# First pair's q and k in three parts, a new order of the attention steps, and the last block copied whole

## The chip, the cores and the metric

One core of one Trainium2 chip runs the whole program. The metric is the time of one execution in device microseconds (us). The engines are named as in the profile: PE (TensorE; PEld its weight loads), DVE (VectorE), ACT (ScalarE), POOL (GpSimd) and SP (SyncE, which issues most DMAs).

## The reference

```python
# q, k, v: (2, 12, 448, 64) f32; tokens 2*448 = 896, d_model 12*64 = 768
scores = q @ k.T / 8;  causal mask;  attn = softmax(scores);  a = attn @ v
x = a.transpose(0, 2, 1, 3).reshape(896, 768)
h = x @ w_in            # 768 x 2048, float64 in memory
x = max(0.01 * h, h) @ w_out          # 2048 x 768
xn = x / sqrt(mean(x*x) + 1e-6) * rms_g
y = (silu(xn @ w_gate) * (xn @ w_val)) @ w_out2    # 768 x 1536, twice, and 1536 x 768
```

## The kernel before, in words

Every product that needs more than fp32r is made of three products of a high and a low part (`prod`, L150). After the attention the program is a long chain of such matmuls on PE: x·w_in, g·w_out, the gated pair, and the last product (L626 to L656), which leaves the output in 14 blocks of 128 rows x 384 columns. Weights come as float64 and are decoded by ACT, DVE and POOL (L96 to L145).

The attention works on 12 pairs of heads (p = 0 to 11). Its steps are small functions, one entry each in a dictionary; the string `ORDER` (L40) lists them, and the program is emitted in that order, engine by engine in first-in-first-out queues. A name is a letter for the step, the pair, and a part; what follows an @ is the engine (A for ACT, D for DVE, P for POOL). The steps that matter here:

- `q`, `k`: load of a pair's q or k into a tile `n` (four buffers). For pair 0 (`PLAIN`, L32) the load, the turn and the copy go by parts: `load_part` (L255), `turn_part` (L265), `copy_part` (L271), with `PARTS` (L34) naming the chunks of 128 rows in each part; q comes through ACT's queue, k through SP's (L263).
- `tq`, `tk`: PE transposes into PSUM (L269 for pair 0, L306 and L309 otherwise; the tile is `qk`, three buffers). `hq`, `hk`: the copy to SBUF (`F`; L275 for pair 0, L315 otherwise). `lq`, `lk`: the low part, on DVE (L319).
- `s`: scores on PE (L331 for pair 0, L345 otherwise; four PSUM buffers). `m`: mask and row maximum on DVE (L353). `e`: exponential on ACT (L362). `g`, `i`, `n`: guard (L367), inverse (L371), normalisation (L375).
- `t`, `c`: PE transposes of the probabilities (`pt`, L382) and their copies (`pT`, L395). `x`: times v on PE (L404). `f`: copy (L412) and low part (L414) of the result; x has one PSUM buffer, so x of pair p waits for f of pair p-1.
- `b`, `d`, `v`: loads of tails of q (tile `qe`, L287), tails of v (`ve`, L291) and of v (`vn`, L282). `w`, `y`, `z`: decode and first matmuls (L421 to L423) of the w_in product, placed among the attention steps. `w0.0` is the DMA of the first 768 KB of w_in (tile `raw`, L104).
- `~n`: n matmuls on a constant tile that only keep PE at work (`keep_busy`, L510); the order of before has none, but 13 stand ahead of the first step (L514). The constant tile `pace` is set by a DVE memset (L86).

Of the kernel before, what the change touches and what calls it, by code (L numbers as in the profile page):

```python
# [37 lines left out]
ORDER = """  # L40
q0a k0a tk0a q0b tq0a hk0a@A tq0b hq0a@A k0b tk0b k1 s0.0 hk0b@A hq0b@A q1 b0 m0.0 s0.2 q2 s0.6 tk1 m0.1 e0.1
k2 m0.3 e0.0 m0.2 g0.0@P m0.6 tq1 e0.3 hk1@A hq1@A i0.0 s0.4 tq2 e0.6 lk1 g0.6@P lq1 m0.4 m0.5 e0.2 hq2@A s1.0
i0.6 lq2 m1.4 m1.0 e0.4 e0.5 m1.1 s1.2 n0.6@P g0.2@P tk2 q3 i0.2 m1.2 hk2@A t0.3 e1.0 c0.3@A k3 tq3 s1.6 lk2
n0.1@P g0.4@P n0.0@P tk3 n0.2@P m1.5 i0.4 q4 tq4 n0.3@P n0.4@P hq3@A e1.4 m1.6 s2.2 d0 m1.3 hk3@A k4 lq3 lk3
hq4@A q5 m2.2 v0 s2.0 e1.3 lq4 b1 e1.6 n0.5@P e1.5 t0.1 c0.1@A k5 t0.2 s2.6 c0.2@A t0.0 e1.1 e1.2 tk4 tq5 m2.4
m2.0 m2.5 m2.1 m2.3 m2.6 s3.2 g1.0@D i1.0 n1.4@D n1.5@D s3.0 hk4@A c0.0@A e2.3 e2.2 m3.2 q6 hq5@A x0 n1.3 n1.2
n1.6@P n1.0 m3.3 lk4 m3.0 t1.3 n1.1 t1.1 e2.0 e2.1 e2.4 m3.5 lq5 m3.1 t1.0 e2.5 e2.6 c1.0@A f0.0@A s3.6 c1.3@D
c1.1@D g2.0@D m3.4 t1.2 tk5 e3.3 tq6 i2.0 s4.0 c1.2@A e3.5 m3.6 n2.5@D hq6@A f0.1 hk5@D n2.4@P n2.3 s4.2 n2.1
x1 e3.1 n2.6@P n2.0 e3.4 q7 m4.0 lk5 n2.2 m4.3 e3.2 e3.6 e4.3 t2.3 m4.5 v1 k6 lq6 m4.1 k9 t2.1 t2.2 e3.0 c2.3@A
m4.4 c2.2@A s4.6 t2.0 w0.0 c2.1@D e4.0 g3.0@P e4.5 c2.0@A d1 q8 f1.0@D m4.2 tk6 i3.0 tq7 hk6@A s5.0 n3.4@P m4.6  # L50
f1.1 e4.4 hq7@D s5.2 n3.6@P m5.1 e4.2 x2 n3.2 lk6 n3.3 e4.1 e4.6 lq7 m5.4 m5.2 n3.5@P n3.1 g4.0@D m5.0 k7 t3.2
n3.0 i4.0 f2.0@A w0.1@P e5.1 e5.4 n4.2 t3.3 n4.0 t3.1 s5.6 c3.2@D c3.3@A n4.6@P c3.1@A f2.1 m5.5 e5.2 tk7 t3.0
hk7@A c3.0@A w0.2 m5.3 m5.6 t4.3 s6.0 m6.0 k8 c4.3@A s6.2 e5.0 n4.4@P e5.6 e5.3 w1.0 n4.3 n4.5@P w0.3 n4.1 lk7
e5.5 x3 t4.1 f3.0@A v2 m6.4 m6.2 w0.4 g5.0@P m6.5 m6.1 i5.0 f3.1 m6.3 n5.1 n5.0 e6.4 c4.1@A s6.6 t4.2 t4.0 tk9
c4.2@A s7.6 c4.0@A hk9@A tk8 tq8 q9 e6.5 m7.6 m6.6 lk9 s7.0 hk8@A e6.0 e6.3 k10 s7.2 hq8@A m7.0 m7.2 n5.3
n5.6@P n5.4@P n5.2 n5.5@P e6.6 e6.2 e6.1 e7.0 x4 lk8 lq8 f4.0@A t5.0 m7.1 m7.4 e7.6 m7.5 w0.5@P t5.3 c5.3@A
t5.1 c5.0@D c5.1@A s8.6 g6.0@D m7.3 f4.1 e7.3 e7.5 t5.2 tq9 i6.0 m8.6 c5.2@D e8.6 e7.4 n6.4@P s8.0 n6.5@P s8.2
n6.1 m8.2 n6.3 n6.0 e7.2 m8.4 m8.3 n6.2 m8.0 hq9@A e7.1 k11 x5 q11 q10 t6.0 n6.6@P lq9 m8.5 m8.1 c6.0@A t6.1
t6.3 t6.2 c6.3@A g7.0@P f5.0@D c6.2@A e8.1 c6.1@D i7.0 f5.1 s9.0 n7.4@D m9.5 m9.4 w0.6 m9.0 s9.2 n7.5@P e8.5
e8.0 e8.2 x6 tq10 tk10 e8.4 v3 m9.1 m9.3 e9.5 e8.3 n7.3 g8.0@P s9.6 hq10@A y0.0 tq11 n7.1 n7.0 m9.2 i8.0 lq10  # L60
f6.0@A hk10@A e9.3 y0.1 n7.2 lk10 n8.0 e9.2 n7.6@D e9.0 hq11@D t7.1 n8.2 n8.5@P lq11 n8.1 n8.3 n8.4@P w1.1@P
t7.3 m9.6 s10.6 c7.1@A y0.2 c7.3@A t7.0 f6.1 t7.2 tk11 y0.3 c7.0@D t8.2 y0.4 e9.6 c7.2@A e9.4 m10.6 w1.2 w1.3
e9.1 t8.1 g9.0@P y0.5 s10.0 z0.0 c8.1@A c8.2@A i9.0 s10.2 hk11@D w1.4 lk11 m10.0 n9.4@P n8.6@P z0.1 w1.5@P x7
m10.1 m10.2 n9.1 t8.0 t8.3 e10.6 m10.4 e10.0 e10.4 n9.2 n9.6@P e10.2 c8.3@A m10.5 s11.6 f7.0@D n9.3 f7.1 s11.0
m10.3 c8.0@A m11.6 s11.2 w1.6 x8 e10.3 m11.5 e10.1 m11.4 e10.5 g10.0@D n9.5@P e11.5 e11.6 i10.0 m11.0 m11.1
t9.3 n10.6@D n9.0 e11.0 c9.3@D n10.4@P e11.4 w2.0 t10.3 y1.0 n10.1 n10.0 t9.2 g11.4@D e11.1 c10.3@A c9.2@A
n10.5@P n10.2 n10.3 y1.1 t9.0 m11.3 f8.0@D i11.4 g11.0@D t9.1 g11.6@D f8.1 i11.6 t10.0 c9.1@A y1.2 w2.1@P
c9.0@D x9 m11.2 t10.2 e11.3 z0.2 w2.2 e11.2 n11.6@P g11.2@P c10.0@D i11.2 f9.0@D f9.1 t10.1 c10.2@A i11.0
n11.4@P t11.3 y1.3 c10.1@A n11.3@P c11.3@D x10 f10.0@A n11.2@P n11.5@P n11.0@D n11.1@P t11.2 t11.1 c11.2@A
t11.0 c11.1@A c11.0@A y1.4 y1.5 z1.0 f10.1 x11 f11.0@A z1.1 w2.3 f11.1 w2.4 z1.2  # L70
"""
# [615 lines left out]
```

## Time and profile before

| | |
|---|---|
| median of 3 runs | 589.68 us (589.66 to 590.01) |
| the profiled execution, its own time | 591.03 us |
| its span, first to last instruction | 589.1 us |
| PE busy | 583.2 us (99%) |
| DVE, ACT, POOL busy | 389.6, 265.1, 49.9 us |
| attention, on PE | from the start to about 96 us |

In the rows, a time is the start in us from the span's start, the next number how long it lasted; in brackets stands how long the engine had been idle and who ended it. `x8` is a count. SPq and ACTq are DMA issues of those engines. Rows of the chain of waits have start, length, and what was waited for.

### The profile page before, as it was taken

To read this page: it belongs to the slowest core of one execution; us is meant where nothing else is said; L and a number is where in the kernel's file an instruction comes from. 1 tells how busy PE (TensorE), PEld (TensorE's weight loads), DVE (VectorE), ACT (ScalarE), POOL (GpSimd) and SP (SyncE) were. 2 spreads that over 40 slices of the span, in tenths; PEclk is the share of its full clock that TensorE was granted. 3 is DMA by queue.
4 is the path that set the end of the run, shared out by engine and by line. 5 is a ranking of instruction groups with operands and counts; after the bars stand their busy time and mean duration, and the time that the engine had idled before them with its cause. 6 is when DMAs were issued, how large, how long until landed. Compare 5 with 4: busy or idle time off the path is not lost.

```text
span 589.1 us, 8454 instructions
## 1 busy us (share of the span) xinstructions
PE 583.2 (99%) x3265; PEld 532.7 (90%) x3265; DVE 389.6 (66%) x703; ACT 265.1 (45%) x521; POOL 49.9 (8%) x105
## 2 busy tenths in 40 slices
PE   8999999999999999999999999999999999999997
PEld 6778878999999999999999999999999999999997
DVE  6989996766666556555655998788787796840000
ACT  6989884444444433332333743434434444420000
POOL 4455570000000000000000000000000000000000
PEclk9999999999999999999999999999999999999999
DMA  7893313433333322333234254344343351721001
GB/s 160 188 219 73 92 55 105 118 110 110 112 121 108 111 92 90 107 106 128 90 107 112 104 160 151 114 132 139 108 145 124 108 160 55 193 75 41 28 27 41
DMA packets 83688, 65.07 MB, mean 110 GB/s; under 512 B 35648, under 2 KB 80576, under 8 KB 83648
## 3 DMA queue, kind: packets, MB, share of 16 engines
q1 hardware_dynamic: 82544, 64.21, 37.7%
q8 instruction: 26, 0.43, 0.3%
q10 hardware_dynamic: 1104, 0.33, 0.2%
q14 instruction: 14, 0.11, 0.1%
HBM read 61.77 MB, written 2.75 MB: 110 GB/s over the span
## 4 chain that ended last, share of the span: by engine, by line
PE 96%; DMA 2%; DVE 1%; SPq 0%; issue 0%; ACTq 0%; ACT 0%
PE mm L541 17%; PE mm L153 10%; PE mm L155 10%; PE mm L154 10%; PE mm L559 7%; PE mm L560 7%; PE mm L558 7%; PE mm L639 5%; PE mm L641 5%; PE mm L640 5%; PE x L404 4%; PE pt L382 3%; PE s L345 3%; DMA n<-in_q_dram 1%; PE qk L306 1%; DMA qe<-in_q_dram 0%
## 5 line engine op out<-in xcount | busy, mean ns | idle before, releaser
L153 PE MATMUL mm<-a,hi 128*128 128x448 f32 x300 | 109.7, 366 | 0.0
L154 PE MATMUL mm<-a,lo 128*128 128x448 f32 x300 | 109.6, 365 | 0.0
L155 PE MATMUL mm<-a,hi 128*128 128x448 f32 x300 | 109.6, 365 | 0.0
L134 ACT CAST hi<-we 128x768 fp32r<-128x768 f32 (+1 forms) x58 | 47.2, 815 | 131.9 <-PE mm L541 53.9
L140 DVE TENSOR_TENSOR lo<-we,hi 128x768 fp32r<-128x768 f32 (+1 forms) x60 | 55.8, 930 | 64.0 <-ACT hi L134 63.9
L123 DVE SCALAR_TENSOR_TENSOR we<-we,ws 128x768 int32<-128x768 int32 (+1 forms) x70 | 65.4, 935 | 28.6 <-ACT we L112 26.5
L541 PE MATMUL mm<-a,hi 128*128 128x448 f32 x336 | 81.8, 365 | 0.0
L112 ACT ACTIVATE we<-raw 128x768 f32<-128x768 f32 (+1 forms) x67 | 59.4, 887 | 39.0 <-DVE lo L140 26.1
L541 PEld LDWEIGHTS mm<-a,hi 128*128 128x128 f32 x336 | 63.2, 188 | 4.9
L127 DVE SCALAR_TENSOR_TENSOR we<-raw,we 128x768 int32<-128x768 int32 (+1 forms) x70 | 65.5, 935 | 1.5
L558 PE MATMUL mm<-b,hi 128*128 128x448 f32 x168 | 61.4, 365 | 0.0
L560 PE MATMUL mm<-b,lo 128*128 128x448 f32 x168 | 61.4, 365 | 0.0
L559 PE MATMUL mm<-b,hi 128*128 128x448 f32 x168 | 61.4, 365 | 0.0
L153 PEld LDWEIGHTS mm<-a,hi 128*128 128x128 f32 x300 | 56.4, 188 | 4.5
L155 PEld LDWEIGHTS mm<-a,hi 128*128 128x128 f32 x300 | 56.4, 188 | 4.4
L154 PEld LDWEIGHTS mm<-a,lo 128*128 128x128 f32 x300 | 56.4, 188 | 4.4
L541 PE MATMUL mm<-a,lo 128*128 128x448 f32 x168 | 47.7, 365 | 0.0
L362 ACT ACTIVATE p<-p,st 128x384 f32<-128x384 f32 (+3 forms) x84 | 44.2, 536 | 1.2 <-DVE st L353 1.2
L119 DVE TENSOR_SCALAR ws<-raw 128x768 int32<-128x768 uint32 (+1 forms) x70 | 38.1, 544 | 7.7 <-DMA raw<-in_moe_w_in_dram 3.0
L654 DVE COPY o<-mm 128x384 f32<-128x384 f32 (+1 forms) x7 | 3.7, 527 | 59.2 <-PE mm L641 53.1
L375 POOL TENSOR_SCALAR p<-p,st 128x384 f32<-128x384 f32 (+3 forms) x77 | 39.0, 525 | 23.4 <-DVE st L371 11.5
L560 PEld LDWEIGHTS mm<-b,lo 128*128 128x128 f32 x168 | 31.6, 188 | 2.5
(135 smaller groups left out, 939.7 us busy)
## 6 DMA issues: line engine op xcount, KB each, us to landing
raw<-in_moe_w_out_dram SPq DMA_DIRECT2D x24, 768.0 KB, 4.4
raw<-in_moe_w_in_dram SPq DMA_DIRECT2D x16, 768.0 KB, 4.7
raw<-in_moe_w_gate_dram SPq DMA_DIRECT2D x12, 768.0 KB, 4.3
raw<-in_moe_w_val_dram SPq DMA_DIRECT2D x12, 768.0 KB, 4.4
raw<-in_moe_w_out_dram SPq DMA_DIRECT2D x6, 512.0 KB, 3.6
out_dram<-o SPq DMA_DIRECT2D x13, 192.0 KB, 1.9
n<-in_k_dram SPq DMA_DIRECT2D x22, 112.0 KB, 3.0
vn<-in_v_dram SPq DMA_DIRECT2D x12, 192.0 KB, 4.4
```

The source lines that it names most:

```text
L112: ACT.activation(out=out, in_=src, func=AF.Copy, scale=2.0 ** -112)
L123: DVE.scalar_tensor_tensor(out=L["e"], in0=L["e"], scalar=3, in1=L["s"], op0=ALU.logical_shift_left, op1=ALU.bitwise_or)
L127: DVE.scalar_tensor_tensor(out=L["e"], in0=L["w"][:, :, 1], scalar=-0x80000000, in1=L["e"], op0=ALU.bitwise_and, op1=ALU.bitwise_or)
L134: ACT.copy(out=L["hi"], in_=L["e"].bitcast(F32))
L140: DVE.tensor_tensor(out=L["lo"], in0=L["e"].bitcast(F32), in1=L["hi"].bitcast(F32), op=ALU.subtract)
L153: PE.matmul(ps, wh, ah, start=(i == 0), stop=False)
L154: PE.matmul(ps, wl, ah, start=False, stop=False)
L155: PE.matmul(ps, wh, al, start=False, stop=(i == n - 1))
L541: PE.matmul(pss[b], w, cols(xT[kk], b)[part], start=kk + part == 0 and w is wh, stop=kk == KC - 1 and w is wl)
L558: PE.matmul(pss[b], wh, ah, start=(f == 0), stop=False)
L559: PE.matmul(pss[b], wh, al, start=False, stop=False)
L560: PE.matmul(pss[b], wl, ah, start=False, stop=(f == NF1 - 1))
```

## The change

It splits pair 0's q and k into three parts (a and b of one chunk of 128 rows each, c of the last two) and copies each by itself, mostly on DVE; the keep-busy matmuls read a constant that the framework sets at the start, 9 of them ahead of the first step and 5 more inside the order; the order of all attention steps is another one; and the last output block is copied whole by ACT and stored by one DMA.

```diff
-PARTS = {"a": (0, 1), "b": (2, 3)}
+PARTS = {"a": (0,), "b": (1,), "c": (2, 3)}
...
-q0a k0a tk0a q0b tq0a hk0a@A tq0b hq0a@A k0b tk0b k1 s0.0 hk0b@A hq0b@A q1 b0 m0.0 s0.2 q2 s0.6 tk1 m0.1 e0.1
...
+q0b q0a tq0a q0c hq0a@D tq0b tq0c k0a ~2 tk0a k0c hq0c@D hq0b@D tk0c hk0a@A hk0c@D k0b tk0b hk0b@A s0.0 k1 b0
+s0.2 m0.1 m0.0 e0.1 s0.4 m0.3 q1 k2 m0.2 tk1 e0.0 g0.0@P e0.3 e0.2 m0.4 e0.4 ~2 tq1 q2 hq1@A hk1@D q3 k3 m0.5
...
-        pace = const.tile([P, 2 * P], mybir.dt.bfloat16, name="pace")
-        DVE.memset(pace, 1.0)
+        pace = nc.const_aps.tensor(1.0, [P, 2 * P], mybir.dt.bfloat16)
...
-            keep_busy(13)
+            keep_busy(9)
...
-                cuts = [0, HALF // 2, HALF] if (nh, t) == (1, T // P - 1) else [0, HALF]
-                for i, (lo, hi) in enumerate(zip(cuts, cuts[1:])):
-                    o = mx.tile([P, HALF], F32, tag=f"t{2 * i}", name="o")[:, lo:hi]
-                    if (t + i) % 2 == 0:
-                        ACT.copy(out=o, in_=ps[:, lo:hi])
-                    else:
-                        DVE.tensor_copy(out=o, in_=ps[:, lo:hi])
-                    (ACT if i == 0 and len(cuts) > 2 else SP).dma_start(
-                        out=out[t * P:(t + 1) * P, nh * HALF + lo:nh * HALF + hi], in_=o)
+                o = mx.tile([P, HALF], F32, tag="t0", name="o")
+                if t % 2 == 0:
+                    ACT.copy(out=o, in_=ps)
+                else:
+                    DVE.tensor_copy(out=o, in_=ps)
+                SP.dma_start(out=out[t * P:(t + 1) * P, nh * HALF:(nh + 1) * HALF], in_=o)
```

Counted over the whole order, DVE has 11 of the `h` copies instead of 4 (four of them the small ones of pair 0), 7 `f` copies instead of 5, 8 normalisations instead of 7 and 5 guards instead of 8; of the 48 `c` copies it keeps 12.

**First place: PE at the start.** Before, from the last keep-busy matmul (`warm`) through the transposes of pair 0 (L269; `n_133` is its k, `n_130` its q), its scores (L331) and the first transposes of pair 1 (L306):

```order
L512 MATMUL warm_115<-pace_68 128x256
L269 MATMUL qk_136<-ident_93,n_133 128x128 x2
L269 MATMUL qk_141<-ident_93,n_130 128x128 x2
L269 MATMUL qk_146<-ident_93,n_130 128x128
L269 MATMUL qk_146<-ident_93,n_130 128x64
L269 MATMUL qk_152<-ident_93,n_133 128x128
L269 MATMUL qk_152<-ident_93,n_133 128x64
L331 MATMUL s_158<-F_144 128x128
L331 MATMUL s_160<-F_144 128x128
L331 MATMUL s_172<-F_144 128x256
L331 MATMUL s_174<-F_144 128x256
L331 MATMUL s_179<-F_144 64x448 x2
```

The same place in the change (`n_124` is the q, `n_138` the k):

```order
L512 MATMUL warm_113<-const-bfloat16-1.0 128x256
L269 MATMUL qk_127<-ident_91,n_124 128x128
L269 MATMUL qk_133<-ident_91,n_124 128x128
L269 MATMUL qk_135<-ident_91,n_124 128x128
L269 MATMUL qk_135<-ident_91,n_124 128x64
L512 LDWEIGHTS const-bfloat16-1.0
...
L269 MATMUL qk_142<-ident_91,n_138 128x128
L269 MATMUL qk_148<-ident_91,n_138 128x128
L269 MATMUL qk_148<-ident_91,n_138 128x64
L269 MATMUL qk_154<-ident_91,n_138 128x128
L331 MATMUL s_157<-F_131 128x128
L331 MATMUL s_159<-F_131 128x128
```

q is turned first, parts a, b, c in that order, then two keep-busy matmuls, then k in the order a, c, b; before, half of k came first, then all of q, then the rest of k.

**Second place: DVE at the start.** Before, after the memsets, the row maxima (L353) of pair 0 begin at once:

```order
L86 MEMSET pace_68 128x256
L496 MEMSET qe_98 128x1536
L353 ISA p_169,st_170<-s_158,mask_102 128x128
L353 ISA st_170 128x1
L353 ISA p_169,st_170<-s_160,mask_102 128x128
```

In the change:

```order
L496 MEMSET qe_96 128x1536
L275 COPY F_131<-qk_127 128x128
L275 COPY F_131<-qk_135 128x192
L275 COPY F_131<-qk_133 128x128
L275 COPY F_131<-qk_148 128x192
L353 ISA p_170,st_171<-s_159,mask_100 128x128
```

Four copies of pair 0 (parts a, c, b of q, part c of k) now stand on DVE ahead of the first row maximum.

**Third place: SP, around the first load of w_in.** Before (`raw_612` is that load, `n_691` the k of pair 7, `n_620` the q of pair 8):

```order
L253 DMA n_580<-in_k_dram 112x4x64 x2
L253 DMA n_585<-in_k_dram 112x4x64 x2
L104 DMA raw_612<-in_moe_w_in_dram 128x6x128
L291 DMA ve_100<-in_v_dram 64x12x64
L253 DMA n_620<-in_q_dram 128x3x64 x2
L253 DMA n_691<-in_k_dram 112x4x64 x2
L253 DMA n_768<-in_k_dram 112x4x64 x2
L104 DMA raw_785<-in_moe_w_in_dram 128x6x128
```

In the change (`n_579` is the k of pair 7, `n_582` its q, `vn_619` the v of pairs 3 to 5, `n_676` the q of pair 8):

```order
L253 DMA n_573<-in_q_dram 128x3x64 x2
L253 DMA n_579<-in_k_dram 112x4x64 x2
L253 DMA n_582<-in_q_dram 128x3x64 x2
L104 DMA raw_617<-in_moe_w_in_dram 128x6x128
L282 DMA vn_619<-in_v_dram 128x6x64 x3
L104 DMA raw_623<-in_moe_w_in_dram 128x6x128
L253 DMA n_676<-in_q_dram 128x3x64 x2
```

The k of pair 7 stands ahead of the first load of w_in instead of behind it; two such loads and a v stand together behind it.

## Rows read from the trace of the kernel before

**Rows 1.** By stretch: length; PE, PEld, DVE, ACT, POOL busy; clock, DMA share, GB/s.

```profile
10.00:20.00 10.00, 9.81 (x90) 8.28 (x88) 10.00 (x42) 9.91 (x31) 4.08 (x10) 1.00 0.86 188
...
30.00:40.00 10.00, 9.28 (x83) 7.72 (x83) 9.71 (x32) 8.99 (x30) 6.58 (x13) 1.00 1.09 205
40.00:97.00 57.00, 57.00 (x477) 44.77 (x476) 50.02 (x153) 45.75 (x134) 29.79 (x58) 1.00 0.32 77
97.00:585.70 488.70, 488.59 (x2484) 459.23 (x2482) 305.45 (x430) 185.05 (x282) 0.00 (x0) 1.00 0.35 109
```

**Rows 2.** PE's timeline, first 12 us.

```profile
1.17 2.96 PE L512 MATMUL warm<-pace 128*128 128x256 bf16 x13 [1.17 <-DVE pace L86]
3.92 2.25 PE L269 MATMUL qk<-ident,n 128*128 128x128 f32 x8
5.90 0.98 PE L331 MATMUL s<-F 64*128 64x128 f32 x8
...
7.95 0.94 PE L306 MATMUL qk<-ident,n 112*128 112x112 f32 x7
```

**Rows 3.** The chain of waits, first 12 us.

```profile
1.25 3.01 DMA n<-in_q_dram
```

**Rows 4.** DMA issues by line: KB each, median us from issue to landing.

```profile
out_dram<-o SPq DMA_DIRECT2D x13, 192.0 KB, 1.9
...
out_dram<-o SPq DMA_DIRECT2D x1, 96.0 KB, 1.6
...
n<-in_q_dram ACTq DMA_DIRECT2D x1, 32.0 KB, 2.8
```

**Rows 5.** DVE's timeline, first 13 us.

```profile
6.61 0.29 DVE L353 CUSTOM_DVE_ANT_0 p<-s,mask 128x128 f32<-128x128 f32 x1 [3.88 <-PE s L331]
...
8.17 0.62 DVE L353 CUSTOM_DVE_ANT_0 p<-s,mask_tail 128x448 f32<-128x448 f32 x1 [0.36 <-PE s L331]
...
9.16 0.62 DVE L319 TENSOR_TENSOR F<-qk,F 128x448 fp32r<-128x448 f32 x1 [0.28 <-ACT F L315]
9.99 0.69 DVE L319 TENSOR_TENSOR F<-qk,F 128x512 fp32r<-128x512 f32 x1 [0.21 <-ACT F L315]
...
11.55 0.16 DVE L371 RECIPROCAL st<-st 128x1 f32<-128x1 f32 x1
```

**Rows 6.** The timeline's end.

```profile
585.67 0.32 ACT L652 COPY o<-mm 128x192 f32<-128x192 f32 x1 [12.01 <-PE mm L641]
...
586.02 0.36 DVE L654 COPY o<-mm 128x192 f32<-128x192 f32 x1 [6.08 <-ACT o L652]
586.41 0.33 SPq L655 DMA_DIRECT2D out_dram<-o  x1
```

**Rows 7.** DVE's groups by shape, 0 to 97 us: busy us, mean ns.

```profile
L412 DVE CAST a<-x 128x448 fp32r<-128x448 f32 x5 | 3.1, 620 | 0.2 <-PE x L404 0.2
...
L315 DVE CAST F<-qk 128x448 fp32r<-128x448 f32 x2 | 1.2, 590 | 0.0
```

**Rows 8.** PE's timeline, 37 to 50 us.

```profile
37.77 0.84 PE L345 MATMUL s<-F 128*128 128x448 f32 x3
39.33 0.57 PE L306 MATMUL qk<-ident,n 112*128 112x112 f32 x4 [0.72 <-DVE st L353]
...
42.12 1.84 PE L404 MATMUL x<-pT,vn 128*64 128x448 f32 x12
```

**Rows 9.** DVE's timeline around 38 us.

```profile
38.23 0.61 DVE L414 TENSOR_TENSOR a<-x,a 128x448 fp32r<-128x448 f32 x1
```

**Rows 10.** SP's timeline from 27 us.

```profile
29.41 0.49 SPq L104 DMA_DIRECT2D raw<-in_moe_w_in_dram  x1
...
32.85 3.96 SPq L253 DMA_DIRECT2D n<-in_k_dram  x4
```

**Rows 11.** DMAs issued from 32.7 to 35.6 us: KB each, median us to landing.

```profile
n<-in_k_dram SPq DMA_DIRECT2D x2, 112.0 KB, 5.8
```

**Rows 12.** ACT's output copies: min/median/max ns.

```profile
L652 ACT COPY o<-mm x8: 318/478/479, 508.7 to 585.7; 128x384 f32<-128x384 f32 x7, 128x192 f32<-128x192 f32 x1
```

More of the change, by code (lines that the diff above doesn't have):

```diff
@@ L40 @@
 ORDER = """
-q0a k0a tk0a q0b tq0a hk0a@A tq0b hq0a@A k0b tk0b k1 s0.0 hk0b@A hq0b@A q1 b0 m0.0 s0.2 q2 s0.6 tk1 m0.1 e0.1
[L42 to L70, printed above, removed]
+q0b q0a tq0a q0c hq0a@D tq0b tq0c k0a ~2 tk0a k0c hq0c@D hq0b@D tk0c hk0a@A hk0c@D k0b tk0b hk0b@A s0.0 k1 b0
@@ new lines @@
+s0.2 m0.1 m0.0 e0.1 s0.4 m0.3 q1 k2 m0.2 tk1 e0.0 g0.0@P e0.3 e0.2 m0.4 e0.4 ~2 tq1 q2 hq1@A hk1@D q3 k3 m0.5
+lk1 i0.0 s0.6 e0.5 lq1 m0.6 g0.4@P g0.2@P d0 n0.0@P tk2 hk2@A ~1 tq2 s1.2 s1.0 i0.2 i0.4 k4 lk2 hq2@A n0.2@P
+tq3 e0.6 n0.3@P n0.4@P m1.3 m1.2 n0.5@P lq2 s1.6 tk3 g0.6@P e1.2 e1.3 hq3@A t0.1 n0.1@P m1.4 m1.1 m1.0 s2.0
+e1.4 m1.5 m1.6 hk3@A q4 lq3 lk3 e1.0 c0.1@A s2.2 t0.2 e1.5 v0 m2.4 i0.6 m2.0 t0.0 c0.2@A m2.3 tq4 m2.1 c0.0@A
+e1.1 s2.6 m2.5 m2.2 m2.6 e1.6 n0.6@P tk4 k5 t0.3 g1.0@D s3.0 i1.0 hk4@D hq4@D e2.0 c0.3@A lk4 e2.6 e2.1 lq4
@@ new lines @@
+e2.2 e2.4 e2.3 n1.0 n1.6@P n1.4@P e2.5 n1.2 n1.5@D s3.2 n1.1 n1.3 x0 t1.3 t1.0 c1.3@A c1.0@A m3.2 t1.1 m3.4
+f0.0@D m3.0 g2.0@P c1.1@A q5 m3.3 m3.1 e3.1 t1.2 k6 b1 s3.6 m3.5 tk6 tq5 i2.0 c1.2@D n2.5@P m3.6 e3.0 hk6@A
+hq5@A e3.3 f0.1 lk6 tk5 n2.2 n2.6@P e3.6 e3.5 s4.0 s4.2 lq5 hk5@D m4.1 x1 m4.4 n2.1 n2.3 n2.4@P t2.3 e3.2 q6
+e3.4 e4.1 n2.0 k7 q7 m4.5 m4.0 g3.0@D t2.2 c2.3@A lk5 t2.0 s4.6 c2.2@A t2.1 c2.0@A f1.0@D i3.0 e4.4 n3.3 n3.0
+w0.0 v1 w1.0 tq6 tq7 m4.2 f1.1 m4.6 m4.3 e4.5 c2.1@D s5.0 n3.5@P n3.6@P m5.4 hq7@A n3.2 n3.4@P s5.2 m5.3 m5.1
@@ new lines @@
+m5.2 n3.1 q8 m5.0 x2 t3.1 e4.0 hq6@A e4.2 lq6 m5.5 e4.6 e4.3 lq7 e5.4 w0.1@P w0.2 f2.0@D t3.3 s5.6 c3.1@A
+c3.3@A t3.2 c3.2@A t3.0 tk7 g4.0@P i4.0 m5.6 f2.1 s6.0 c3.0@A e5.5 n4.1 n4.2 e5.1 s6.2 e5.0 x3 e5.3 n4.5@P e5.6
+e5.2 hk7@D m6.4 n4.3 n4.4@P t4.2 m6.5 n4.0 n4.6@P g5.0@P m6.2 m6.1 m6.3 m6.0 e6.5 lk7 s6.6 t4.1 t4.0 i5.0
+n5.6@P c4.2@A e6.3 e6.4 t4.3 f3.0@D s7.6 m6.6 c4.0@A c4.1@D m7.6 c4.3@A e6.0 t5.3 tq8 k8 tk8 f3.1 n5.1 hq8@A
+e6.6 n5.3 n5.5@P n5.0 c5.3@A hk8@A s7.0 w0.3 m7.5 s7.2 m7.4 lq8 m7.1 e6.1 x4 n5.4@P n5.2 t5.1 e6.2 q9 t5.0 m7.0
@@ new lines @@
+g6.0@D lk8 i6.0 t5.2 f4.0@A s8.6 e7.6 c5.1@A m7.2 w0.4 c5.0@A k9 k10 v2 d1 k11 m7.3 m8.6 f4.1 e7.4 e7.5 c5.2@A
+tq9 tk9 hq9@D n6.4@P hk9@A e7.3 e7.0 e7.1 n6.3 lq9 s8.0 s8.2 m8.4 q10 n6.6@P n6.0 m8.2 e7.2 lk9 x5 g7.0@D m8.0
+i7.0 w0.5@P n6.1 n6.2 m8.5 m8.3 m8.1 t6.3 n6.5@P f5.0@A c6.3@A n7.1 f5.1 t6.1 t6.2 t6.0 n7.3 n7.4@P e8.4 c6.0@A
+c6.1@D c6.2@A e8.1 e8.6 n7.6@D s9.0 s9.2 x6 w0.6 m9.0 n7.5@D m9.1 m9.4 m9.5 v3 e8.0 e8.5 t7.3 tq10 q11 e8.3
+c7.3@A tk11 e8.2 hk11@A w1.1@A m9.2 m9.3 hq10@D s9.6 tk10 hk10@A y0.0 lq10 g8.0@P n7.2 lk11 i8.0 m9.6 lk10 tq11
@@ new lines @@
+n8.4@P n7.0 y0.1 n8.5@P hq11@A e9.0 e9.3 t7.1 y0.2 lq11 n8.6@D t7.0 t7.2 y0.3 w1.2 c7.0@D c7.2@D f6.0@A e9.4
+c7.1@A e9.1 e9.6 s10.6 t8.3 n8.1 y0.4 n8.0 c8.3@A e9.2 n8.3 n8.2 t8.0 t8.2 w1.3 m10.6 t8.1 y0.5 e9.5 c8.1@A
+w1.4 g9.0@P s10.0 z0.0 w1.5@P c8.2@D f6.1 s10.2 m10.0 m10.5 i9.0 x7 c8.0@A e10.6 f7.0@A m10.4 m10.3 m10.1 n9.2
+n9.6@P e10.4 n9.3 m10.2 f7.1 e10.2 e10.1 e10.5 n9.4@P n9.1 s11.2 w1.6 n9.5@P n9.0 e10.0 e10.3 s11.0 m11.1 m11.2
+m11.4 x8 t9.3 m11.5 t9.2 t9.1 s11.6 e11.4 g10.0@P m11.3 i10.0 c9.3@A f8.0@A c9.2@D c9.1@D m11.0 f8.1 t9.0 n10.3
@@ L71 @@
+y1.0 n10.6@P n10.2 e11.5 e11.3 e11.2 t10.3 n10.4@P c9.0@D g11.4@P g11.2@P i11.4 z0.1 y1.1 n10.0 n10.5@P c10.3@D
+x9 w2.0 m11.6 i11.2 t10.2 n11.3@D n11.4@D e11.1 y1.2 e11.6 e11.0 n11.2@P n10.1 g11.6@P f9.0@D t10.1 t10.0
+g11.0@D n11.5@D c10.2@A i11.6 f9.1 t11.1 c10.1@D c10.0@A n11.6@P c11.1@A i11.0 n11.1@P y1.3 x10 n11.0@D t11.0
+t11.2 w2.1@P c11.0@A t11.3 c11.2@A y1.4 c11.3@A w2.2 f10.0@D w2.3 f10.1 y1.5 z1.0 x11 z1.1 z1.2 f11.0@D z0.2
+w2.4 f11.1
 """
```

## The prediction

> **What bounds the kernel now.** I read the stretches first. From 97 us on PE is busy 488.59 of 488.70 us [rows 1], with the same matmuls in the changed kernel, so nothing can be won there: what changes is the time at which the attention hands PE over, and the tail behind the last matmul. In the attention PE is also full, except at the start, in the stretch to 20 us (9.81 of 10) and in that to 40 us (9.28 of 10) [rows 1]. So a gain has three places: the start, the holes up to 40 us, the tail. The second thing to see in the same rows is who could take PE's place: from 10 to 20 us DVE is busy 10.00 and ACT 9.91 of 10 us, while from 40 to 97 us DVE has 57.00 - 50.02 = 7.0 us free. Next I read the start engine by engine [rows 2 to 5], then the end [rows 6], then the hole at 39 us [rows 8 to 11].
>
> About 0.2% (1.2 us) is what a measurement of this kernel can tell from no change.
>
> **The tail: 0.** Before, ACT copies a half from 585.67, DVE the other behind it, and the last store is issued at 586.41 [rows 6] and takes 1.6 us [rows 4]: landed at 588.0. In the change ACT copies all 384 columns, 0.48 us like the seven others [rows 12], until 586.15; the store follows some 0.03 later (the gap between the DVE copy's end, 586.38, and its store) and, with 192 KB, takes 1.9 [rows 4]: 588.1. Two halves in a row against one longer copy and one longer store: between 0 and +0.1 us, taken as 0.
>
> **The start: 0, between -0.1 and +1.4.** PE no longer waits for a memset until 1.17 us [rows 2]; the other engines begin at 0.7 to 0.8, so its 9 keep-busy matmuls, each (3.92 - 1.17)/13 = 0.21 us, run from some 0.9 to 2.8. But the next instruction now turns part a of q, the second load on ACT's queue. Before, the second load was issued at 1.25 and took 3.01 [rows 3], so it lands at 4.26; the two loads have the same size. Before, PE turned k first, at 3.92 [rows 2]. The early warm-up thus ends in an idle stretch of 4.3 - 2.8 = 1.5 us. The 32 KB tail of q is the fourth load; ACT issues them some 0.53 us apart, so at 2.3, and it takes 2.8 [rows 4]: 5.1. Then come two keep-busy matmuls (to about 5.75) and k's transposes. PSUM has three buffers for these tiles, so k's part c waits until DVE has copied q's part c: turned by 5.55, plus 0.36, the time of a DVE copy of 192 columns [rows 6], is 5.95. DVE then copies q's part b (0.3, by the same row) and k's part c (0.36, turned by about 6.55), and the first row maximum follows at about 6.95, where before it started at 6.61 [rows 5]. So the three parts do not bring the maxima forward; they bring them 0.35 us later.
>
> DVE gives that back. From 6.61 to 11.55 it made seven maxima, two low parts and a reciprocal, with 0.36 + 0.28 + 0.21 = 0.85 us of holes [rows 5], that is 4.1 us of work. The changed order gives it those, plus the copy of pair 1's k (0.59 [rows 7], on ACT before), 4.7 us, and its inputs are there in time: the two wide maxima, not the tail's, come right behind the first four. 6.95 + 4.7 = 11.65 against 11.55, with ACT relieved of 0.5. I take 0. Below: if the loads land 0.1 earlier. Above: TensorE's clock (a rival, below).
>
> **The holes up to 40 us: -0.9, between -1.2 and 0.** After the three matmuls from 37.77 PE is idle 0.72 us until 39.33 [rows 8]; by the pace of matmuls of this width, 488.59/2484 = 0.197 us [rows 1], the three were issued by 38.36, which makes 0.97. The rows name a maximum on DVE, but what PE turns there is the k of pair 7. That k stands behind the first 768 KB of w_in, issued at 29.41; SP issues its two loads from 32.85 on [rows 10], they take 5.8 us each [rows 11], and the second, issued about 33.7, lands at 39.2 to 39.5: that is what PE waits for. In the change it stands ahead of the w_in load and the wait goes. I take 0.9, nearer to the pace than to the modelled ends. In the stretch to 20 us 0.2 is idle as well [rows 1]; the load that is waited for there is now used later by PE, but DVE is full, so I count it only in the lower end: -0.97 - 0.2 = -1.2. Nothing is won if another wait takes the hole's place; that is the upper end.
>
> What is late next? Two w_in loads and one v now stand together, ahead of pair 8's q. The v is needed by x of pair 3, which began at 42.12 [rows 8]; issued around 30, with the 5.8 us that loads took in that crowd plus one w_in load of 768 KB at 205 GB/s [rows 1], 3.7 us, it lands by 39.5. Pair 8's q is turned behind pair 5's first transposes, some 3 us later still. Both covered.
>
> **More work on DVE: 0, up to +0.9.** DVE gets three large copies more (seven, less the four small ones of the start) at 0.59, two f copies at 0.62 [rows 7], a normalisation at about 0.5, and gives back three guards at about 0.2: 1.8 + 1.2 + 0.5 - 0.6 = 2.9 us in all. Counted by the order's steps, 1.7 us of it stand between the first maximum and the f of pair 2, on which x of pair 3 waits. Before, that f ended at 38.23 + 0.61 = 38.84 [rows 9], so it now ends near 40.6; x of pair 3, with the hole gone, is wanted at 41.2. That fits, with half a microsecond to spare; the rest lies in the 7.0 us that DVE has free after 40 us [rows 1]. If that cover fails, the gain of 0.9 is lost.
>
> The 5 keep-busy matmuls in the order (5 x 0.11 = 0.55 us at full pace, half that of the start) stand where PE waits for loads or copies: 0.
>
> **Sum.** Against the profiled execution (span 589.1, its own time 591.03): 0 + 0 - 0.9 + 0 = -0.9 us, so a span of 588.2. That execution took 1.35 us more than the median of the runs shown; the difference carries over: 589.68 - 0.9 = **588.8 us**.
>
> **The rivals.**
>
> *ACT was the bound of the first 30 us.* ACT is as full as DVE from 10 to 20 us [rows 1] and before 30 us loses three copies of q and k and one f copy and gains one copy of probabilities, net three at about 0.5 us. If PE waited for ACT there and not for DVE, up to 1.5 us comes on top; with 1.0 of it, 587.8. Against it: DVE has no hole at all in that stretch, and gets more.
>
> *The hole moves.* DVE, with 2.9 us more, becomes what x of pair 3 or of pair 7 waits for, or the crowded loads are late. Then the 0.9 is given back: 589.7.
>
> *The clock comes late (slower).* The eight transposes from 3.92 take 2.25 us, 0.28 each, the seven from 7.95 only 0.94, 0.13 each [rows 2]: TensorE went from 1.2 to 2.4 GHz in between, after running from 1.17 without a hole. From 10 us on the granted clock is 1.00, the higher level [rows 1]. In the change PE has a hole of 1.5 us ahead of its first transposes. If the rise is put off by that, the scores and transposes that took 0.98 + 0.94 us at full pace [rows 2] take twice that, +1.9, and about 0.5 of it hides behind the loads: +1.4, in a place where DVE and then ACT are full and can't catch up. 588.8 + 1.4 = 590.2, or 591.1 if the hole at 39 us isn't won either. It decides from the point where pair 1's k is turned: still 0.2 us per transpose there, and this case is in. For it speaks the hole; against it, that PE had run for longer by then (from 0.9). The Trainium skill, page TensorE: Matmul & The Clock Gate, section Part 1: The HAM clock gate, says that the lower clock is the default state and that sustained activity releases it; by that rule fewer and earlier warm-up matmuls with a hole behind them are a step back, and the time would be this rival's. That the rise came behind an unbroken run agrees with it; no run here shows what a hole does.
>
> **How the numbers follow.** The forecast has 0.45, ACT as the bound 0.2, the moved hole 0.2, the late clock 0.15. The forecast's own range is 588.3 to 589.3; a third of it lies under 588.5, all of the ACT case does: faster 0.35. Of the clock case about half lies over 590.9, and a little of the moved hole: slower 0.1. The rest, 0.55, is within 0.2%. The range for 8 in 10 goes from the ACT case, 587.8, to the lower clock figure, 590.3.
>
> **What would show it.** Right: the first transpose near 4.3 and the first maximum near 6.9; DVE without holes from there to 11.6; no idle PE at 38 to 40 us, and x of pair 3 some 0.9 us earlier than 42.1; the last store issued near 586.2 less the gain, 1.9 long. Wrong: transposes of pair 1 at 0.2 us each; PE waiting for DVE ahead of x of pair 3 or 7; an end of attention that moves by more than 1.5 us either way, which would mean that ACT or DVE, and not one load, set the pace.

## The result, and the profile after

The change makes the kernel slower: 593.00 us median of 6 runs (592.79 to 593.83), beside 589.81 us (589.66 to 590.01) for the kernel before; the ratio is 1.0056, 95% interval 1.0043 to 1.0068, that is +3.2 us where -0.9 was forecast and 590.3 was the range's upper end. The profiled execution of after took 593.09 us, almost its median, with a span of 591.2.

The stretches of after, against [rows 1]:

```profile
10.00:20.00 10.00, 10.00 (x88) 8.22 (x88) 9.42 (x38) 8.58 (x26) 3.96 (x10) 1.00 0.88 165
...
30.00:40.00 10.00, 9.91 (x87) 7.63 (x87) 8.92 (x37) 9.04 (x29) 5.32 (x11) 1.00 1.00 243
40.00:97.00 57.00, 56.05 (x473) 44.27 (x473) 50.50 (x156) 46.98 (x139) 31.25 (x59) 1.00 0.38 82
97.00:585.00 488.00, 488.00 (x2487) 458.31 (x2484) 307.95 (x434) 185.33 (x282) 0.00 (x0) 1.00 0.35 109
```

The hole of 30 to 40 us is all but gone, as forecast (9.91 of 10 us; experiment 5 asks whether the change took it away). But DVE and ACT, both full from 10 to 20 us before, now have 0.6 and 1.4 us free there: something feeds them too slowly. And PE, full from 40 to 97 us before, has lost 0.95 us. These are the two places to look at.

PE's timeline of the first 12 us of after, against [rows 2]:

```profile
0.76 2.08 PE L512 MATMUL warm<-const-bfloat16-1.0 128*128 128x256 bf16 x9 [0.76 <-PEq L668]
4.10 1.21 PE L269 MATMUL qk<-ident,n 128*128 128x128 f32 x4 [1.26 <-POOL mask_tail L502]
...
6.90 3.18 PE L331 MATMUL s<-F 64*128 64x128 f32 x12
10.01 1.01 PE L306 MATMUL qk<-ident,n 112*128 112x112 f32 x4
...
11.08 0.49 PE L306 MATMUL qk<-ident,n 128*128 128x128 f32 x3
```

The nine warm-up matmuls end at 2.84 us, and PE stands idle for 1.26 us; the row names a POOL instruction as the releaser, but the part of q that is turned landed at 3.96, and that is what PE waited for. The twelve score matmuls of pair 0 then take 3.18 us, and four transposes of pair 1's k 1.01 us. In [rows 2] seven such transposes took 0.94: this is the lower clock, 1.2 GHz instead of 2.4. The trace's record of the granted clock begins with a step up to full, at 10.90 us in after and at 5.89 us in the profiled execution of before; it holds nothing ahead of that step, so the stretches read 1.00 throughout, and that the clock was at its lower level until then is read from these paces. The first maximum on DVE starts at 7.87 us, where [rows 5] had 6.61:

```profile
7.87 0.29 DVE L353 CUSTOM_DVE_ANT_0 p<-s,mask 128x128 f32<-128x128 f32 x1 [0.91 <-PE s L331]
```

PE's timeline from 39 us, against [rows 8], has no idle time left; pair 7's k is turned at 41.14 without waiting:

```profile
39.58 0.84 PE L345 MATMUL s<-F 128*128 128x448 f32 x3
40.27 1.03 PE L382 MATMUL pt<-ident,p 128*128 128x128 f32 x8
41.14 0.55 PE L306 MATMUL qk<-ident,n 112*128 112x112 f32 x4
...
43.02 1.84 PE L404 MATMUL x<-pT,vn 128*64 128x448 f32 x12
```

The new loss lies near 72 us. In PE's timeline:

```profile
71.17 0.60 PE L382 MATMUL pt<-ident,p 128*128 128x128 f32 x4
...
72.32 0.66 PE L382 MATMUL pt<-ident,p 128*128 128x128 f32 x4
73.92 0.76 PE L382 MATMUL pt<-ident,p 128*128 128x128 f32 x5 [0.95 <-POOL p L375]
```

and in POOL's, in three narrow stretches (the second row groups two normalisations, of which the later starts at 72.24; the last is the one that PE waits for):

```profile
68.87 0.38 POOL L375 TENSOR_SCALAR p<-p,st 128x128 f32<-128x128 f32 x1
...
71.87 0.85 POOL L375 TENSOR_SCALAR p<-p,st 128x128 f32<-128x128 f32 x2 [2.62 <-PE pt L382]
...
72.69 1.17 POOL L375 TENSOR_SCALAR p<-p,st 128x256 f32<-128x256 f32 x1
```

POOL had been idle for 2.62 us, waiting for PE's transposes of 71.17, and PE then waits for POOL. Both work on the same tile, pair 8's probabilities: in the new order `t8.3` stands ahead of `n8.1`, `n8.0`, `n8.3` and `n8.2`. The first of these, of other columns, does not wait: it is the row of 68.87, ahead of the transposes of 71.17. `n8.0` does, and the kernel shows a reason. The tail's block lies in columns 0 to 447 (L230, `OFF`), but the last of its four transposes reads 128 columns from 384 on (L382), and so the first 64 of block 0, which begins at 448 and which `n8.0` writes. `n8.3` and `n8.2` stand behind `n8.0` in POOL's queue. No run here narrowed that transpose, so that `n8.0` waits for this overlap is read from the kernel and the rows, not tested. In the order of before all of pair 8's normalisations that `t8.0` to `t8.2` need stood ahead of its first transposes.

The end of the timeline, against [rows 6] and [rows 12]. PE's last row in before is

```profile
585.25 0.34 PE L641 MATMUL mm<-hi,b 128*128 128x384 f32 x1
```

and in after, with what follows it,

```profile
587.34 0.34 PE L641 MATMUL mm<-hi,b 128*128 128x384 f32 x1
587.75 0.48 ACT L650 COPY o<-mm 128x384 f32<-128x384 f32 x1 [12.01 <-PE mm L641]
588.26 0.33 SPq L653 DMA_DIRECT2D out_dram<-o  x1
```

From PE's last matmul to the last record it is 591.21 - 587.34 = 3.87 us; before it was 589.12 - 585.25 = 3.87.

When x of a pair starts on PE (us) shows where the time goes; the last three columns are runs from below:

| pair | before | after | before, second profile | after, 16 warm-ups | with norms moved too |
|---|---|---|---|---|---|
| 0 | 21.35 | 22.76 | 21.19 | 21.19 | 21.13 |
| 2 | 34.60 | 36.85 | 34.60 | 35.28 | 35.17 |
| 3 | 42.12 | 43.02 | 41.23 | 41.47 | 41.34 |
| 6 | 60.88 | 62.16 | 59.97 | 60.60 | 60.49 |
| 11 | 93.79 | 95.87 | 92.91 | 94.28 | 92.88 |

### The profile page after: what moved, and what is told of

Same layout as the page of the kernel before. It is cut to its first block, busy times and chain, and to the rows that moved or that the text cites. A ratio compares the mean times of both kernels' runs of the same rounds, so it can differ in the third digit from the quotient of the medians.

```text
span 591.2 us, 8441 instructions
## 1 busy us (share of the span) xinstructions
PE 584.6 (99%) x3266; PEld 533.5 (90%) x3266; DVE 390.7 (66%) x708; ACT 264.0 (45%) x515; POOL 50.5 (9%) x106
## 4 chain that ended last, share of the span: by engine, by line
PE 98%; POOL 1%; issue 0%; ACT 0%; POOLq 0%; ACTq 0%
PE mm L541 17%; PE mm L153 10%; PE mm L155 10%; PE mm L154 10%; PE mm L559 7%; PE mm L560 7%; PE mm L558 7%; PE mm L639 5%; PE mm L641 5%; PE mm L640 5%; PE x L404 4%; PE pt L382 4%; PE s L345 4%; PE qk L306 1%; PE s L331 1%; POOL p L375 0%
## 5 line engine op out<-in xcount | busy, mean ns | idle before, releaser
L362 ACT ACTIVATE p<-p,st 128x256 f32<-128x256 f32 (+3 forms) x84 | 44.0, 530 | 2.3 <-DVE st L353 2.3
L119 DVE TENSOR_SCALAR ws<-raw 128x768 int32<-128x768 uint32 (+1 forms) x70 | 37.9, 542 | 8.4 <-DMA raw<-in_moe_w_gate_dram 3.1
L375 POOL TENSOR_SCALAR p<-p,st 128x256 f32<-128x256 f32 (+3 forms) x76 | 40.2, 548 | 24.7 <-DVE st L371 17.1
L652 DVE COPY o<-mm 128x384 f32<-128x384 f32 x6 | 3.3, 555 | 53.0 <-PE mm L641 53.0
```

## The experiments

**Theory.** Two separate costs: the hole ahead of the first transposes puts off the rise of TensorE's clock, and pair 8's normalisations stand in the wrong place. **Rivals.** The order and the three parts cost the time by themselves, through DVE; or the repairs only uncover the next wait.

**1. The start filled up (changed kernel).**

```diff
-            keep_busy(9)
+            keep_busy(16)
```

> The changed kernel with 16 warm-up matmuls ahead of the first transpose instead of 9 (at 0.21 us each they reach to about 4.1 us, where the first part of q lands). Theory (the late clock): the 1.26 us in which PE stands idle from 2.84 to 4.10 put TensorE's rise off to 10.9 us; without them it comes near 6 us as before, the scores of pair 0 run at full pace, and what x of pair 0 to 2 starts late (1.4 to 2.3 us) comes back: 590.7 to 591.6. Rival (the new order and the three parts cost the time themselves): 592.7 to 593.2, as the changed kernel, whatever the clock does.

Measured: 591.51 us median, ratio to the kernel before 1.0026 (1.0015 to 1.0037). PE's timeline:

```profile
4.13 1.24 PE L269 MATMUL qk<-ident,n 128*128 128x128 f32 x4
...
6.75 2.14 PE L331 MATMUL s<-F 64*128 64x128 f32 x12
8.82 0.61 PE L306 MATMUL qk<-ident,n 112*128 112x112 f32 x4
```

The clock steps up at 6.37 us, the scores take 2.14 us instead of 3.18, and 1.5 us come back, though the order is the new one. The theory holds for this half.

**2. The kernel before with the changed warm-up alone.**

```diff
-        pace = const.tile([P, 2 * P], mybir.dt.bfloat16, name="pace")
-        DVE.memset(pace, 1.0)
+        pace = nc.const_aps.tensor(1.0, [P, 2 * P], mybir.dt.bfloat16)
...
-            keep_busy(13)
+            keep_busy(9)
```

> The kernel before with only the warm-up changed: the framework's constant and 9 matmuls instead of 13, the order as it was. Theory (the late clock): the hole ahead of the first transpose, some 1.1 us, puts the rise off to 10 us or later, and the time goes up by 1.0 to 2.3 us: 590.8 to 592.1. Rival (the new order costs the time): 589.6 to 590.0, no change, with the rise near 6 us still or its cost hidden behind DVE.

Measured: 591.41 us median (590.27 to 592.34), ratio 1.0018 (1.0005 to 1.0030). The clock steps up at 11.35 us:

```profile
2.96 0.45 PE L268 MATMUL qk<-ident,n 128*128 128x128 f32 x1
3.77 2.35 PE L268 MATMUL qk<-ident,n 128*128 128x128 f32 x7 [0.36 <-DMA n<-in_k_dram]
5.76 3.43 PE L330 MATMUL s<-F 64*128 64x128 f32 x12
9.13 1.65 PE L305 MATMUL qk<-ident,n 112*128 112x112 f32 x7
```

The same loss with the old order, 1.2 us. Here one transpose stands in the hole, and 0.12 and 0.36 us of idle time are left of it; the step is late all the same.

**3. The normalisations moved (changed kernel).**

```diff
-s10.6 t8.3 n8.1 y0.4 n8.0 c8.3@A e9.2 n8.3 n8.2 t8.0
+s10.6 n8.1 n8.0 n8.3 n8.2 t8.3 y0.4 c8.3@A e9.2 t8.0
```

> The changed kernel with three normalisations of pair 8 on POOL moved ahead of the tail's transposes of that pair, so that they no longer wait for PE to have read the same tile. Theory (POOL waits for PE and then PE for POOL, 0.95 us idle at 73 us): 593.0 - 0.95 = 592.0, x of pair 7 starting about 1 us earlier. Rival (the time is hidden by another wait, or DVE's copies take the place): 592.8 to 593.2.

The edit moves `n8.1` along with the three that waited. Measured: 591.91 us, ratio 1.0027 (1.0017 to 1.0037), with the clock's step at 11.10 us. PE is busy 57.00 of 57 us from 40 to 97 us, and the median is 1.1 us lower.

**4. Both repairs.** The edits of 1 and 3 together.

> The changed kernel with both repairs, 16 warm-up matmuls and the three normalisations of pair 8 ahead of the tail's transposes. Theory (late clock and POOL wait are separate and together all that the change costs): ratio to the kernel before 1.0056 - 0.0030 - 0.0029 = 0.9997, some 590.0 where the kernel before has 590.2. Rival (they overlap, or a further cost stands behind them): 591.0 or more, the ratio over 1.0015.

Measured: 590.01 us median, ratio 1.0000 (0.9991 to 1.0008). The clock steps up at 6.30 us; POOL no longer waits between pair 8's normalisations and the guard of pair 9, and PE turns the tail and the first two groups without a break:

```profile
67.53 1.80 POOL L375 TENSOR_SCALAR p<-p,st 128x128 f32<-128x128 f32 x3
71.97 0.24 POOL L367 TENSOR_SCALAR st<-st 128x7 f32<-128x7 f32 x1 [2.64 <-ACT p L362]
```

```profile
69.51 0.60 PE L382 MATMUL pt<-ident,p 128*128 128x128 f32 x4
...
70.56 1.47 PE L382 MATMUL pt<-ident,p 128*128 128x128 f32 x12
```

593.00 to 591.51 by the warm-up, to 590.01 by the normalisations: 1.5 + 1.5 us, all that the change had cost (the kernel before measured 589.81 to 590.18 beside these runs; the ratios, each to the kernel before of the same time, fall by 0.0030 and 0.0026). The traces agree on the second part: from x of pair 6 to x of pair 7 PE takes 14.81 and 14.79 us without the moved normalisations, 13.49 and 13.50 with them, so 1.3 us. Taken together, the three parts, the copies on DVE, the rest of the order and the whole last copy are worth nothing that can be measured, either way; none of them was run by itself.

**5. Was the hole at 39 us there in other executions?** The kernel before, unchanged, profiled twice more.

> The kernel before, unchanged, once more with a profile. Theory (the hole of 0.72 to 0.97 us at 38 to 39 us belongs to that one profiled execution, whose own time of 591.03 lay 1.35 us over the median): own time 589.7 to 590.2, PE without a hole from 30 to 40 us, x of pair 3 at about 41.4 instead of 42.12. Rival (the hole stands in every execution, and the 1.35 us are something else): the hole is there at the same size whatever the time.

> A second look at the kernel before, unchanged, for the same question: with the hole at 38 to 39 us if its own time is near 591, without it if it is near 590 (theory); with it in either case (rival).

Measured: 590.04 and 590.25 us. In the first, the stretch and PE's timeline against [rows 1] and [rows 8]:

```profile
30.00:40.00 10.00, 10.00 (x92) 8.53 (x91) 9.86 (x34) 9.44 (x33) 6.90 (x14) 1.00 1.00 236
```

```profile
37.77 0.85 PE L345 MATMUL s<-F 128*128 128x448 f32 x3
38.45 0.55 PE L306 MATMUL qk<-ident,n 112*128 112x112 f32 x4
38.84 1.04 PE L382 MATMUL pt<-ident,p 128*128 128x128 f32 x8
```

No hole; x of pair 3 starts at 41.23. The second profile has none either: pair 7's k, landed at 38.88 and 39.20 in the execution that the prediction rests on, is there at 36.37 and 36.66. So the hole was real, and its end fits the late load (the second part landed 0.13 us ahead of the transposes), but it belonged to one execution in which that load came late; of the three profiled ones it is the only one with the hole.

**6. The load moved (kernel before).**

```diff
-k6 lq6 m4.1 k9 t2.1
+k6 lq6 m4.1 k7 t2.1
...
-m5.0 k7 t3.2
+m5.0 k9 t3.2
```

> The kernel before with the loads of pair 7's k and pair 9's k exchanged in the order, so that pair 7's k stands ahead of the first load of w_in; nothing else. Theory (PE's 0.97 us of idle time from 38.4 is the wait for that load alone): 589.8 - 0.9 = 588.9, x of pair 3 starting 0.9 us earlier than 42.1. Rival (the hole moves, or the maximum on DVE that the rows name is what PE waited for): 589.6 to 590.0.

Measured: 590.10 us, ratio 1.0003 (0.9993 to 1.0012). Pair 7's k now lands by 31.7 us, PE is full from 30 to 40 us and x of pair 3 starts at 41.41, but so it does, at 41.23 and 41.47, in the two profiles of experiment 5. The measurement falls in the rival's range, for neither of the reasons given there: nothing moves, there was nothing to win.

**7. Number, start or hole?** Two warm-ups with the old order. First 15 matmuls from the constant:

```diff
-        pace = const.tile([P, 2 * P], mybir.dt.bfloat16, name="pace")
-        DVE.memset(pace, 1.0)
+        pace = nc.const_aps.tensor(1.0, [P, 2 * P], mybir.dt.bfloat16)
...
-            keep_busy(13)
+            keep_busy(15)
```

> The kernel before with the framework's constant and 15 warm-up matmuls, which run from 0.76 to about 3.9 us without a hole. Theory (what counts for the clock is that PE has no hole up to its first transposes, and its rise follows the start of the unbroken run): the rise at 5.9 us or up to 0.4 earlier, the time 589.8 to 590.2 where the kernel before has 590.0 to 590.2. Rival (the framework's constant itself, or the earlier start, puts the rise off): 591 or more, as with 9.

Measured: 590.08 us, ratio 0.9995 (0.9987 to 1.0004), the step at 5.55 us. That is within the theory's range: the framework's constant does no harm and wins nothing. Then 7 matmuls that start late:

```diff
-        DVE.memset(pace, 1.0)
...
             DVE.memset(qe, 0.0)
+            DVE.memset(pace, 1.0)
...
-            keep_busy(13)
+            keep_busy(7)
```

> The kernel before with its memset of the warm-up's tile behind that of qe, so that the warm-up starts about 1.3 us later, and with 7 matmuls instead of 13, which again end where the first transposes begin (about 4.0 us). Fewer warm-up matmuls than the changed kernel's 9, but no hole. Theory (the unbroken run counts): the rise comes some 4.7 us after the run's start, as in the kernel before (1.17 to 5.89), so near 7.2 us, and the time goes up by 0.4 to 0.8 us: 590.4 to 590.8. Rival (the number of warm-up matmuls counts): the rise near 11 us as with 9, and the time 591.2 or more.

Measured: 590.26 us, ratio 1.0002 (0.9991 to 1.0013), the step at 6.01 us:

```profile
2.78 1.68 PE L512 MATMUL warm<-pace 128*128 128x256 bf16 x7 [2.78 <-DVE pace L496]
4.25 2.14 PE L268 MATMUL qk<-ident,n 128*128 128x128 f32 x8
6.12 0.98 PE L330 MATMUL s<-F 64*128 64x128 f32 x8
...
8.17 0.93 PE L305 MATMUL qk<-ident,n 112*128 112x112 f32 x7
```

Both expectations miss: the rise is neither 4.7 us behind the start of the run (7.5) nor late. Seven matmuls that start at 2.78 do as well as thirteen from 1.17, and better than nine from 0.76 that end at 2.84. In these runs the late step goes with the break ahead of the transposes, not with the number of matmuls or the time of the first one.

**8. A shorter hole (changed kernel).** `keep_busy(13)` in place of 9.

> The changed kernel with 13 warm-up matmuls: they end near 3.6 us, and a hole of 0.3 to 0.5 us is left ahead of the first transpose, where the changed kernel has 1.26 and the one with 16 none. Theory (the hole decides, not the number): either the rise is near 6.4 us and the time 591.5, as with 16, if so short a hole is borne, or near 11 us and 593.0, as with 9; a rise in between (7 to 9 us) speaks for the rival, that each missing matmul puts it off by its share.

Measured: 592.37 us median, ratio 1.0036 (1.0024 to 1.0048), in two groups: seven executions at 591.30 to 592.37 and five at 593.64 to 593.95. The profiled one, 592.37:

```profile
0.76 2.91 PE L512 MATMUL warm<-const-bfloat16-1.0 128*128 128x256 bf16 x13 [0.76 <-PEq L668]
4.09 0.41 PE L269 MATMUL qk<-ident,n 128*128 128x128 f32 x2 [0.42 <-POOL mask_tail L502]
4.69 0.66 PE L269 MATMUL qk<-ident,n 128*128 128x128 f32 x2 [0.19 <-DMA n<-in_q_dram]
...
6.53 2.93 PE L331 MATMUL s<-F 64*128 64x128 f32 x12
```

Its clock stepped up at 3.52 us already, was at the lower level again from 6.93 on, after the holes of 0.42 and 0.19 us, and was up for good at 10.35. The two groups of times suggest that the shorter hole is sometimes borne and sometimes not; only this one execution was profiled.

**9. Without the five keep-busy matmuls** (both repairs in, the two `~2` and the `~1` taken out of the order), and the same kernel profiled twice more.

> The changed kernel with 16 warm-up matmuls and the moved normalisations, but without the 5 keep-busy matmuls in its order. Theory (they stand where PE waits and cost nothing, as predicted): 590.0, as with them, the rise near 6.4 us still. Rival 1 (they hold the clock): the rise near 11 us, 591.5. Rival 2 (they stand in PE's way): 589.5 or less.

> The same kernel as the one without the 5 keep-busy matmuls, once more with a profile. Theory (its two groups of times are an early and a late rise of the clock): if its own time is near 590.0, the scores of pair 0 take about 2.1 us and the rise lies before 7 us; if it is near 591.4, they take 3.2 us and the rise lies at 10 us or later. Rival (the rise lies late in every execution without those matmuls, and the two groups have another cause): late rise and 3.2 us also at 590.0.

> A second look for the same question, with the same two answers: near 590.0 with an early rise or near 591.4 with a late one (theory), or late whatever the time (rival).

Measured: 590.09 us median, ratio 0.9997 (0.9986 to 1.0008), eight executions at 589.88 to 590.13 and four at 591.09 to 592.55. The three profiled executions fell among the longer ones:

| own time | granted clock |
|---|---|
| 591.13 | up at 4.54, down again at 7.96 after holes of 0.34 and 0.19 us, up for good at 11.37 |
| 591.43 | up at 10.15 |
| 592.45 | up at 13.12 |

From 10.15 to 13.12 us of waiting for the clock the time grows by 1.02 us, about a third of the delay. The same slope between experiment 1 and after is 1.6/4.5 (own times 591.5 and 593.09, steps at 6.37 and 10.90), and carried back from 10.15 to the 6.3 us of experiment 4 it gives 591.43 - 1.3 = 590.1, where the other group lies. All three, at 591.13 and above, have a late step, as the theory has it; none fell at 590.0, so the early half of it was not seen in this kernel. The profile of 592.45 shows no hole in PE's timeline, but its eight first transposes are spread from 4.13 over 3.01 us, where eight at the lower clock take 2.25 [rows 2]: PE waited between them, and the modelled ends hide it. An unbroken warm-up is thus no guarantee of an early step.

```profile
4.13 3.01 PE L269 MATMUL qk<-ident,n 128*128 128x128 f32 x8
7.07 3.18 PE L331 MATMUL s<-F 64*128 64x128 f32 x12
```

Whether the five matmuls are of use stays open: the medians are alike, and the longer executions without them (591.09 to 592.55) lie above those with them (four of 11 at 590.52 to 590.96), but with them no longer one was profiled.

**10. A version meant to beat both**: 15 warm-ups from the constant, the load of experiment 6, and `b0` ahead of `q1`.

> A version meant to beat both: the kernel before with 15 warm-up matmuls from the framework's constant, pair 7's k loaded ahead of pair 9's and of w_in, and the tails of q (qe) loaded ahead of pair 1's q, since PE waited 0.16 to 0.58 us for qe near 9 us in the looks at the kernel before. Theory (that wait is on the path): the median 0.2 to 0.5 us under the kernel before, 589.5 to 589.8 beside 590.0. Rival (DVE, full from 10 to 20 us, hides it): 590.0, no change.

Measured: 590.08 us, ratio 0.9993 (0.9984 to 1.0002), no difference that can be told. The wait for qe went, and another took its place, now for pair 1's q:

```profile
7.72 0.60 PE L305 MATMUL qk<-ident,n 112*128 112x112 f32 x4
8.77 0.52 PE L305 MATMUL qk<-ident,n 128*128 128x128 f32 x3 [0.45 <-DMA n<-in_q_dram]
```

None of the kernels run is faster than the kernel before by more than can be told.

## Why the prediction was wrong, by its own steps

**The start: 0. This step failed**, and its rival *the clock comes late* is what happened. The times of the rows were well told: the first transpose at 4.10 us (4.3 forecast), a hole of 1.26 us (1.5). The deciding point that was named, pair 1's k still at 0.2 us per transpose, decided: 1.01 us for four. Even the price was near: +1.4 forecast, 1.5 us measured between after and experiment 1. What was wrong is that the step took 0 for it, with a weight of 0.15, and the argument behind that, that PE had run for longer by then. Nine matmuls ahead of a hole did not bring the step forward (11.35 us, experiment 2); seven without one had it at 6.01 (experiment 7). The Trainium skill, page TensorE: Matmul & The Clock Gate, section Part 1: The HAM clock gate, was cited for the lower clock as the default and its release by sustained activity; the runs agree, with the step at 5.89 us behind the unbroken run of before and at 10.90 behind the hole of after.

A smaller miss in the same step: the first maximum was forecast for 6.95 us and came at 7.34 in experiment 4 (7.87 in after). The copies on DVE were told well, they end at 6.52 + 0.36 = 6.88 us there; but the step let the maximum follow them at once, and it waits for the scores on PE, 0.46 us in experiment 4 and 0.91 in after:

```profile
7.34 0.29 DVE L353 CUSTOM_DVE_ANT_0 p<-s,mask 128x128 f32<-128x128 f32 x1 [0.46 <-PE s L331]
```

It is made up later: x of pair 0 starts at 21.13 us in experiment 4, at 21.19 in the second profile of before.

**The holes up to 40 us: -0.9. This step failed in its size**: 0 for the median. The mechanism was right, as the execution with the hole shows; but that execution took 591.03 us, 1.35 more than the median, and the step took the hole out of the median all the same, with the sentence that the difference carries over. Where one profiled execution is slower than the median by more than a hole is long, that hole is the first suspect for the difference.

**More work on DVE: 0.** Right for DVE, which is busy 50.50 of 57 us from 40 to 97 us and is waited for nowhere there. But the count of moved steps went over DVE, ACT and the loads and left out POOL: no term asked on which side of a transpose its normalisations stand, so this cost stood at nothing without a reason. That missing term is the other half of the loss, 1.1 us (experiment 3) to 1.5 us (from experiment 1 to 4). The rivals named DVE and late loads as the wait that could take the hole's place; it was POOL's, in another stretch. The cover that the step named, DVE's 7.0 us free after 40 us, does not cover POOL.

**The tail: 0.** Right: 3.87 us before and after. **Five keep-busy matmuls: 0.** Not contradicted by the medians (experiment 9).

**Sum.** +1.5 for the clock, +1.5 for POOL, 0 for the hole: 3.0, against 3.2 measured. With the clock's rival at its own price of 590.2 to 591.1 and the unseen 1.1 to 1.5 of POOL on top, the prediction's own numbers would have reached 591.3 to 592.6.

## What to carry to other kernels

Let warm-up matmuls end where the first operand lands, not earlier: in these runs a gap behind them cost more than a smaller number of them. In a new order of steps, follow every tile that one engine changes in place while another reads parts of it, column by column: a read that is wider than its data reaches into the neighbouring block, whose write may then have to wait for it, and an idle engine stalls a full one. Before a hole in a profile becomes a term of a forecast for the median, look whether the profiled execution is itself slower than the median.

## What the runs showed of the hardware

**The moment of the rise differs between executions of one program.** The step up that lasted lay at 3.76 to 6.37 us or at 10.15 to 13.12 us in the 16 profiled executions, and never between; three of one program gave 10.15, 11.37 and 13.12. Those with a hole of 1 us or more ahead of the transposes are all of the second kind; those of the second kind do not all have such a hole (experiments 2, 8 and 9). The kernel before has this too, by its times: of its 83 executions beside these experiments 63 took 589.67 to 590.73 us, 19 took 591.19 to 591.57, some 1.4 us more, the price of a late rise, and one 593.24. None of the 19 was profiled, so that they are late rises is an inference. What follows a short hole differs too: after holes of 0.42 and 0.19 us the clock fell back in experiment 8, while in experiment 10 it stepped up at 3.76 us and stayed up over holes of 0.34, 0.17 and 0.45 us.

**POOL's normalisations double beside some DVE instructions.** The one that PE waited for took 1.17 us, where its shape mostly takes 0.48. At 0.48 it would have ended 0.69 us earlier, so by this estimate about 0.26 of PE's 0.95 us of idle time would be left with the order as it is; no run separated the two. All 76 of after (min, median, max ns):

```profile
L375 POOL TENSOR_SCALAR p<-p,st x76: 367/484/1370, 13.6 to 90.8; 128x128 f32<-128x128 f32 x23, 128x256 f32<-128x256 f32 x23, 128x384 f32<-128x384 f32 x20, 128x448 f32<-128x448 f32 x10
```

Five of them take about twice their shape's usual time or more (0.85, 1.17, 1.18, 1.37, 1.37 us), and each of the five overlaps a decode step of the weights on DVE by 0.55 to 0.96 us; here it was

```profile
72.49 1.04 DVE L127 SCALAR_TENSOR_TENSOR we<-raw,we 128x768 int32<-128x768 int32 x1
```

The Trainium skill, page SBUF — State Buffer, section SBUF: two separate sides, says that DVE and GpSimd share one pair of ports, and that a DVE instruction with two inputs in SBUF, if it starts first, takes it for its whole length while the other engine, if it reads SBUF, stands still. Four of the five agree: the decode step beside them reads two tiles, and it starts ahead of the normalisation in three cases and 0.02 us behind it in the fourth; the fifth, of 0.85 us, lies beside one that reads a single tile (L119). No run here took such a step away to test it.
